# Q and K of the strided heads kept in token order, their score products reading both operands with a stride of 16 tokens

## The chip, the cores and the metric

The kernel runs on one core of a Trainium2 chip. The metric is the time of one execution on the device in microseconds (us); for the kernel before, the median of three runs is 591.43 us (590.43 to 592.25). The engines are called PE (TensorE matmuls), PEld (TensorE's weight loads, which overlap the matmuls), DVE (VectorE), ACT (ScalarE), POOL (GpSimd) and SP (SyncE, which issues most transfers).

## The reference, cut to what matters

Eight batches of eight heads, 576 tokens, head dimension 64, all in float32. A sparse attention is followed by a gated feed-forward block with a product over the token dimension:

```python
stride = 32
rel = pos[:, None] - pos[None, :]
mask_local = (rel >= 0) & (rel < stride)
mask_strided = (rel >= 0) & (pos[None, :] % stride == pos[:, None] % stride)
masks = np.stack([mask_local if h < H // 2 else mask_strided for h in range(H)], axis=0)
scores = np.where(masks[None], scale * np.matmul(q, k.transpose(0, 1, 3, 2)), -1e9)
attn = softmax(scores)
attn_out = np.matmul(attn, v)              # 8 heads side by side: x[b, token, 512]

h = gelu(x @ w_in)                         # 512 -> 1024
u, v = h[..., :512], h[..., 512:]
v_n = layernorm(v) * g_ln
v_s = einsum('ts,bsd->btd', w_sg, v_n) + b_sg
out = x + (u * v_s) @ w_out
```

Heads 0 to 3 are local (a token sees the 32 tokens up to itself), heads 4 to 7 strided (a token sees those earlier tokens whose number is the same modulo 32). The kernel groups the strided heads' tokens into 16 classes modulo 16, 36 tokens each. The score product of a class with itself is 36 by 36, and a mask then takes out half of it by parity.

## The kernel before, in words

Heads are handled in four pairs `hh` (0 and 1 local, 2 and 3 strided). The two heads of a pair lie on partitions 0 to 63 and 64 to 127, so every tile of a pair holds both.

For a pair, `qk_load` (step LQ) brings Q and K in as `raw` tiles, 32-token blocks with tokens on partitions. `qk_transpose` (step TQ, lines 425 to 437) turns each with one DVE transpose in 32 by 32 blocks into `qT` and `kT`: head dimension on partitions, 576 tokens along the row. For the strided pairs (lines 435 and 436) the transpose writes through a rearranged view, so that the 36 tokens of a class lie next to each other: inside a 32-token block its output moves on by 36 elements per token. For the local pairs it writes the row straight through.

`strided_scores` (step SS, line 490) makes 32 products per pair: 16 classes by 2 heads, each with 36 columns of `qT` as the weights and 36 columns of `kT` as the moving operand, into one tile `ss`. On the trace each float32 product is two records, so a pair has 64 matmul records and 64 weight loads, and the two heads' products stand side by side in the instruction stream on different halves of the array.

After the scores come the softmax steps: MK adds the mask (DVE, reads `ss`), MX the maximum, SB the subtraction, EX the exponential (ACT), SU the sums, ML the product with the reciprocal (POOL or DVE), then transposes of the probabilities (PS), their copy (CS, ACT) and the product with V (PV, PW) into `os`. XH and XL split the result `os` into two parts of `xt`; for strided pairs they write `xt` through the view `by_class`, which puts class-ordered columns back in token order with a step of 16 elements. XR and XD send it to DRAM for the residual.

The feed-forward part of a batch is made of products with full tiles: `v` (56 matmuls), `u` (96), `sg` (112), `o` (48 or 60), 64 or 128 weight columns, 288 or 512 moving columns.

The order of all work is written out by hand in three strings of steps: START (batch 0's attention, the weights' preparation, batch 0's feed-forward and batch 1's attention), CYCLE (batches 1 to 6: feed-forward of batch b, attention of batch b+1) and LAST (batch 7). In a CYCLE the PE's part is v, local scores, v, u, SS of pairs 2 and 3 back to back, u, sg, o with the attention's products between. TQ of pair 3 stands behind the local scores' mask, TQ of pair 2 behind the layer norm's centring (step lm). Every engine runs its own instructions in this order; no step passes another on the same engine. All calls go through one recording helper, so the profile shows nearly everything as line 81, and instructions are told apart by tiles.

Of the kernel before, what the change touches and what calls it, by code (L numbers as in the profile page):

```python
# [99 lines left out]
def tile_sparse_attention_moe(  # L100
# [17 lines left out]
    B, H, S, D = q.shape  # L118
    P = 128
    DM = H * D  # L120
    NH = DM // P
# [4 lines left out]
    NCL = 16  # L126
    TP = S // NCL
# [22 lines left out]
    def psum(name, own, other):  # L150
        banks, tag = other if alt[0] else own
        return banks.tile([P, 2, 512], F32, tag=tag, name=name)
# [4 lines left out]
    def at_tile(name):  # L157
        return psum(name, (psa, "at"), (psm, "mm"))
# [266 lines left out]
    def qk_transpose(b, hh):  # L425

        for nm in ("q", "k"):
            flat = state[b, hh, "raw" + nm].rearrange("p n d -> p (n d)")
            if nm == "k" and hh < NH // 2:
                dst = state[b, hh, "k"][:, ST : ST + S]  # L430
            else:
                tt = p2.tile([P, S + ST], F32, tag=nm + "T", name=f"{nm}T_{b}_{hh}")
                state[b, hh, nm] = tt
                dst = tt[:, 0:S]
            if hh >= NH // 2:
                dst = dst.rearrange("p (tl tb th) -> p tb th tl", tl=NCL, th=2)
            dve.transpose(dst, flat)

    def v_zeros(b, hh):
# [50 lines left out]
    def strided_scores(b, hh):  # L490
        qT, kT = state[b, hh, "q"], state[b, hh, "k"]
        ps = state[b, "s", hh] = at_tile(f"ss_{b}_{hh}")
        for rb in range(8):
            for n in range(2):
                c = 8 * n + rb
                for hp in range(2):
                    hr = slice(64 * hp, 64 * hp + 64)
                    pe.matmul(
                        ps[64 * hp : 64 * hp + TP, n, rb * TP : rb * TP + TP],
                        qT[hr, c * TP : c * TP + TP],  # L500
                        kT[hr, c * TP : c * TP + TP],
                        start=True, stop=True,
                    )

# [401 lines left out]
    def out_send(b, kk):  # L906
# [7 lines left out]
    STEPS = {  # L914

        "LQ": qk_load, "TQ": qk_transpose, "LV": v_load, "TZ": k_zeros, "LZ": v_zeros, "SL": local_scores,
        "SS": strided_scores, "MK": sm_mask, "MX": sm_max, "SB": sm_sub, "EX": sm_exp,
        "SU": sm_sum, "ML": sm_mul, "PL": local_pt, "CL": local_pt_copy, "CM": local_pt_last,
        "VA": lambda b, hh: local_pv(b, hh, range(NJ)),
# [79 lines left out]
```

## Time and profile before

| | before |
|---|---|
| median of 3 runs | 591.43 us |
| the profiled execution's own time | 591.94 us |
| its span (first to last instruction) | 590.2 us |
| mean granted TensorE clock | 0.984 |
| PE busy | 537.2 us, 91% |
| DVE busy | 412.1 us, 70% |
| ACT busy | 269.4 us, 46% |
| POOL busy | 206.4 us, 35% |

The span falls into three parts. Up to about 60 us the PE is mostly idle while weights are prepared and the first attention is made. From about 60 to 137 us the PE is mostly busy, with some waits. From 137 us on it runs almost without a break to the end. A row of the timeline gives start, duration, engine, operation, output<-inputs, shapes and count; where the engine stood idle before, a bracket tells how long and what ended it. A matmul's duration there holds its way through the pipeline, so the pace of a stream is read from the distance between starts and not from the duration of one.

### The profile page before, as it was taken

The numbers are of one execution on the slowest core, as the hardware profiler recorded it, in microseconds if no ns is written. First come the engines' busy times: TensorE is split into PE (matmuls) and PEld (weight loads), VectorE is DVE, ScalarE is ACT, GpSimd is POOL, SyncE is SP. The second block draws the span as 40 slices with busy tenths as digits, with TensorE's granted clock in tenths as the row PEclk, the third lists the DMA queues.
The fourth block names the chain that finished last, engine by engine and source line by source line (L and its number), as shares of the span: only waits on it lengthen the run. The fifth ranks groups of instructions, "written<-read, shape, count | busy, mean of one in ns | idle before, by whom it ended". The sixth has DMA issues, their size and how long they took to land.

```text
span 590.2 us, 14898 instructions
## 1 busy us (share of the span) xinstructions
PE 537.2 (91%) x6033; PEld 481.4 (82%) x6033; DVE 412.1 (70%) x676; ACT 269.4 (46%) x379; POOL 206.4 (35%) x476
## 2 busy tenths in 40 slices
PE   0344998999999999999999999999999999999996
PEld 0334787988998889978998888988998889988995
DVE  5899999768875587657875587657875587545532
ACT  2455655641572338433562337443662338434320
POOL 6354574630732035300732026310732035302310
PEclk9996799999999999999999999999999999999999
DMA  9998737786852787247832777247932781056002
GB/s 201 177 166 170 148 87 148 143 183 160 175 83 61 160 154 136 41 117 159 167 64 60 160 154 129 41 116 161 171 57 59 162 156 46 0 118 157 0 1 89
DMA packets 281061, 69.94 MB, mean 118 GB/s; under 512 B 266721, under 2 KB 266721, under 8 KB 280994
## 3 DMA queue, kind: packets, MB, share of 16 engines
q1 hardware_dynamic: 199970, 50.12, 41.7%
q10 hardware_dynamic: 81024, 18.89, 15.4%
q8 instruction: 47, 0.77, 0.6%
q14 instruction: 20, 0.16, 0.1%
HBM read 50.09 MB, written 18.87 MB: 117 GB/s over the span
## 4 chain that ended last, share of the span: by engine, by line
PE 65%; DVE 9%; DMA 6%; SPq 5%; ACT 4%; POOL 4%; issue 3%; ACTq 3%; DVEq 0%
PE sg L81 18%; PE o L81 14%; PE v L81 11%; PE u L81 11%; SPq L81 5%; DMA xd<-xs 3%; PE os L81 3%; POOL nt L81 3%; ACTq L81 3%; PE ol L81 2%; PE sa L81 2%; DMA v<-in_v_dram 1%; PE ss L81 1%; DVE cv L81 1%; ACT L81 1%
## 5 line engine op out<-in xcount | busy, mean ns | idle before, releaser
L81 PE MATMUL sg<-wsh,vg 128*128 128x288 f32 x512 | 113.1, 296 | 0.0
L81 PE MATMUL u<-xt,wih 128*128 128x288 f32 x512 | 103.9, 297 | 2.1 <-ACT u L81 2.1
L81 PE MATMUL o<-woh,vg 128*128 128x512 f32 x288 | 95.6, 397 | 0.0
L81 PEld LDWEIGHTS sg<-wsh,vg 128*128 128x128 f32 x512 | 85.6, 188 | 0.5
L81 PE MATMUL v<-wih,xt 128*128 128x512 f32 x256 | 85.0, 402 | 1.0 <-DVE xt L81 1.0
L81 PEld LDWEIGHTS u<-xt,wih 128*128 128x128 f32 x512 | 82.1, 188 | 4.0 <-ACT u L81 2.8
L81 ACT ACT_TABLE_LOAD x40 | 51.3, 1283 | 54.3 <-DMA xd<-xs 26.6
L81 PE MATMUL u<-xt,wil 128*128 128x288 f32 x256 | 75.4, 295 | 0.0
L81 PE MATMUL sg<-wsl,vg 128*128 128x288 f32 x256 | 75.4, 294 | 0.0
L81 PEld LDWEIGHTS o<-woh,vg 128*128 128x128 f32 x288 | 54.1, 188 | 11.2
L81 PEld LDWEIGHTS v<-wih,xt 128*128 128x128 f32 x256 | 48.3, 190 | 13.5 <-DVE xt L81 2.1
L81 PE MATMUL o<-wol,vg 128*128 128x512 f32 x144 | 56.3, 391 | 0.0
L81 DVE TENSOR_TENSOR ob<-o,xn 128x512 f32<-128x512 f32 x32 | 22.0, 691 | 45.4 <-PE o L81 43.0
L81 PE MATMUL v<-wil,xt 128*128 128x512 f32 x128 | 50.6, 395 | 0.0
L81 ACT CAST vg<-gt 128x576 fp32r<-128x576 f32 (+2 forms) x48 | 22.9, 509 | 60.5 <-DVE gt L81 60.5
L81 PEld LDWEIGHTS sg<-wsl,vg 128*128 128x128 f32 x256 | 48.2, 188 | 0.0
L81 PEld LDWEIGHTS u<-xt,wil 128*128 128x128 f32 x256 | 48.0, 188 | 0.0
L81 POOL TENSOR_TENSOR sms<-sms,sr 100x576 f32<-100x576 f32 x15 | 17.5, 1164 | 64.5 <-DVE sr L81 64.5
L81 DVE TENSOR_TENSOR gt<-sg,u 128x576 f32<-128x576 f32 x32 | 23.6, 738 | 22.5 <-PE sg L81 13.7
L81 DVE BATCH_NORM_STATS2 bnst<-hv 128x6 f32<-128x512 f32 (+1 forms) x40 | 27.0, 676 | 17.0 <-ACT hv L81 16.9
L81 PE MATMUL sa<-kT,qT 64*32 64x64 f32 x1024 | 16.4, 244 | 19.5 <-DVE kT L81 19.5
L81 DVE SCALAR_TENSOR_TENSOR vg<-hv,y,vg 128x512 fp32r<-128x512 f32 x32 | 22.5, 746 | 15.4 <-ACT vg L81 15.4
(144 smaller groups left out, 1079.3 us busy)
## 6 DMA issues: line engine op xcount, KB each, us to landing
rawq<-in_q_dram SPq DMA_DIRECT2D x128, 72.0 KB
rawk<-in_k_dram SPq DMA_DIRECT2D x128, 72.0 KB
xd<-xs ACTq DMA_DIRECT2D x128, 72.0 KB
xn<-xd SPq DMA_DIRECT2D x8, 1024.0 KB
out_dram<-ob ACTq DMA_DIRECT2D x32, 256.0 KB
v<-in_v_dram SPq DMA_DIRECT2D x32, 144.0 KB
v<-in_v_dram SPq DMA_DIRECT2D x64, 72.0 KB
stage<-in_moe_w_in_dram SPq DMA_DIRECT2D x8, 512.0 KB
```

The source lines that it names most:

```text
L81: ins = self.tc.keep_in_program_order(op(*args, **kwargs))
```

## The change

Q and K of the strided pairs are transposed into token order, as the local pairs' are. The score products of a class `c` then read the tokens `c`, `c + 16`, `c + 32` and so on directly from the row: both their operands, the weights and the moving one, have a step of 16 elements (64 bytes) between columns. The result `ss` is laid out as before, and nothing behind it is touched.

```diff
@@ qk_transpose
                 dst = tt[:, 0:S]
-            if hh >= NH // 2:
-                dst = dst.rearrange("p (tl tb th) -> p tb th tl", tl=NCL, th=2)
             dve.transpose(dst, flat)
@@ strided_scores
         ps = state[b, "s", hh] = at_tile(f"ss_{b}_{hh}")
+        qc, kc = (x[:, 0:S].rearrange("p (t c) -> p c t", c=NCL) for x in (qT, kT))
         for rb in range(8):
             for n in range(2):
                 c = 8 * n + rb
@@
                     pe.matmul(
                         ps[64 * hp : 64 * hp + TP, n, rb * TP : rb * TP + TP],
-                        qT[hr, c * TP : c * TP + TP],
-                        kT[hr, c * TP : c * TP + TP],
+                        qc[hr, c],
+                        kc[hr, c],
                         start=True, stop=True,
                     )
```

No instruction is added, removed or moved. On the DVE the transposes of the strided pairs keep their place and change their output shape; these rows are the place in START where TQ of pair 3 stands between a softmax's reciprocal (`sr`) and the splitting of a weight tile (`wsl`, `wst`):

```order
 L81 TENSOR_SCALAR sr_4_313<-sr_4_313 128x8
 L81 RECIPROCAL sr_4_313<-sr_4_313 128x8
-L81 STREAM_TRANSPOSE qT_3_328<-rawq_3_317 128x36x16
-L81 STREAM_TRANSPOSE kT_3_330<-rawk_3_322 128x36x16
+L81 STREAM_TRANSPOSE qT_3_328<-rawq_3_317 128x576
+L81 STREAM_TRANSPOSE kT_3_330<-rawk_3_322 128x576
 L81 TENSOR_TENSOR wsl<-wsgT_334,wsh 128x4x128
 L81 TENSOR_TENSOR wst<-wsgT_334,wsh 64x128
```

The neighbours are the same; the strided output 36 by 16 became one run of 576. The PE's list is the same row by row, since only the step inside the operands of the `ss` products differs.

## Prediction

> **What bounds the kernel now.** I read the page first (busy times and the 40 slices), then busy time by stretches, then the PE's timeline around the products that the change touches, then the waits of the PE, and at last the groups of instructions by shape. The page:
>
> ```profile
> span 590.2 us, 14898 instructions
> PE 537.2 (91%) x6033; PEld 481.4 (82%) x6033; DVE 412.1 (70%) x676; ACT 269.4 (46%) x379; POOL 206.4 (35%) x476
> PE   0344998999999999999999999999999999999996
> DVE  5899999768875587657875587657875587545532
> ```
>
> Busy time by stretches, first the preparation, then two of the loop's batches:
>
> ```profile
> 28.80:57.00 28.20, 12.87 (x224) 11.20 (x219) 27.31 (x48) 16.03 (x28) 13.82 (x13) 0.86 0.91 165
> ...
> 137.00:204.50 67.50, 67.26 (x762) 60.34 (x760) 47.65 (x76) 31.20 (x41) 20.93 (x54) 1.00 0.62 125
> 204.50:269.20 64.70, 63.93 (x747) 57.69 (x745) 45.49 (x70) 30.82 (x37) 20.74 (x53) 1.00 0.59 118
> ```
>
> The columns are PE, PEld, DVE, ACT and POOL. From 29 to 57 us DVE is full (27.31 of 28.20 us) and PE is not half busy; in the loop PE is full (67.26 of 67.50 us) and DVE has some 20 us free in a batch. So there are two rules: in the preparation a shorter DVE instruction can count; from about 137 us on only PE time counts, and a saving on DVE counts where PE waits for something behind DVE.
>
> The strided scores on PE's timeline, in START (28.54, 87.90, 94.92) and in a batch of the loop (223.31):
>
> ```profile
> 28.54 2.14 PE L81 MATMUL ss<-kT,qT 64*36 64x36 f32 x64 [4.41 <-DVE kT L81]
> ...
> 87.90 1.31 PE L81 MATMUL ss<-kT,qT 64*36 64x36 f32 x64
> ...
> 94.92 1.31 PE L81 MATMUL ss<-kT,qT 64*36 64x36 f32 x64 [1.79 <-ACT u L81]
> ...
> 100.51 0.74 PE L81 MATMUL wsgT<-ident,wsg 128*128 128x128 f32 x5 [0.90 <-DMA wsg<-in_moe_w_sg_dram]
> 223.31 2.43 PE L81 MATMUL ss<-kT,qT 64*36 64x36 f32 x128
> 225.67 0.54 PE L81 MATMUL u<-xt,wih 128*128 128x288 f32 x2
> ```
>
> In the loop 128 records start between 223.31 and 225.67, 2.36 us. Two records, one per head, stand side by side on the two halves of the array, so there are 64 steps of 36.9 ns; the work before and behind is the `u` product of the same engine, without a bracket: the block lies bare on the path. The chain that ended last holds it as a piece of its own:
>
> ```profile
> 223.38 2.36 PE ss L81 x128
> ```
>
> Six batches of the loop have this block (batches 1 to 6; the last makes no attention), and START has four blocks of 64.
>
> What PE waits for in all:
>
> ```profile
> PE ss L81 <- DVE kT L81: 7.0, 2, 4.4
> ...
> PE u L81 <- ACT u L81: 2.1, 3, 1.1
> PE ss L81 <- ACT u L81: 1.8, 1, 1.8
> ```
>
> The 7.0 us are the two blocks of batch 0, in the preparation. The 2.1 us are three batches of the loop, where the `u` product behind the scores needs a PSUM tile that ACT has not yet emptied.
>
> **The change, part by part: the DVE transposes.** A transposition into a strided output and one straight through:
>
> ```profile
> 219.80 1.25 DVE L81 STREAM_TRANSPOSE qT<-rawq 128x576 f32<-128x576 f32 x1
> 220.90 1.21 DVE L81 STREAM_TRANSPOSE kT<-rawk 128x576 f32<-128x576 f32 x1
> ...
> 239.20 0.77 DVE L81 STREAM_TRANSPOSE qT<-rawq 128x576 f32<-128x576 f32 x1
> 239.90 0.74 DVE L81 STREAM_TRANSPOSE kT<-rawk 128x576 f32<-128x576 f32 x1
> ```
>
> The second pair is the local heads' and has the very form that the strided pairs get. A pair of transposes falls from 2.46 to 1.51 us, by 0.95; sixteen pairs (8 batches, 2 strided pairs of heads) give 15.2 us of DVE time.
>
> In the loop that is 1.9 us a batch on an engine with 20 us free. For it to count, PE must wait behind it, and there it waits in three batches, 2.1 us together. The chain of one of these waits:
>
> ```profile
> 290.80 0.20 POOL y L81
> ...
> 291.02 1.34 ACT vg L81 x2
> ...
> 293.68 0.66 ACT u L81
> ...
> 294.38 3.45 PE u L81 x24
> ```
>
> ACT empties the tile late because it first waits for POOL's chain of the layer norm (step lr, which stands ahead of TQ of pair 2 in the string and so doesn't wait for it). So I take 0 there, with 2.1 us as the other end.
>
> In START four pairs stand, two of them among the full DVE work of the preparation:
>
> ```profile
> 27.17 1.22 DVE L81 STREAM_TRANSPOSE kT<-rawk 128x576 f32<-128x576 f32 x1
> 28.80 0.69 DVE L81 TENSOR_TENSOR wsl<-wsgT,wsh 128x512 fp32r<-128x512 f32 x1 [0.41 <-ACT wsh L81]
> ...
> 35.95 1.21 DVE L81 STREAM_TRANSPOSE qT<-rawq 128x576 f32<-128x576 f32 x1
> ...
> 73.08 1.20 DVE L81 STREAM_TRANSPOSE qT<-rawq 128x576 f32<-128x576 f32 x1
> ```
>
> Behind the first pair DVE had finished `kT` and stood 0.41 us for ACT; ending 0.95 us sooner it would stand 1.36 us. The second pair (35.95 us) is followed by dense work, so its 0.95 us should pass on to the end of the preparation. Two more pairs (from 73.08 us) come where PE is nearly full; what they could free are the waits of 1.79 and 0.90 us above, and the latter is for a transfer. I take 1.0 us for all of START, between 0 and 3.6 (0.95 and these two waits).
>
> **The change, part by part: the strided products.** 36 columns at a step of 64 bytes, on both operands. No matmul or weight load of this kernel reads with such a step, so the price is bounded. From below: nothing. A strided read that costs nothing is in the trace, though from PSUM: `xs<-os` reads with a step, `xs<-ol` straight.
>
> ```profile
> L81 DVE STREAM_TRANSPOSE xs<-os 128x576 f32<-128x576 f32 x16 | 12.5, 778 | 12.7 <-PE os L81 12.7
> L81 DVE STREAM_TRANSPOSE xs<-ol 128x576 f32<-128x576 f32 x16 | 12.4, 774 | 0.1
> ```
>
> From above: accesses to SBUF with the very step of 16 float32 elements, on two engines. `xt<-os` has it (ACT writes with it; DVE reads one operand and writes with it), `xt<-ol` goes straight:
>
> ```profile
> L81 DVE TENSOR_TENSOR xt<-os,xt 128x576 fp32r<-128x576 f32 x16 | 18.2, 1140 | 3.3 <-ACT xt L81 3.3
> L81 DVE TENSOR_TENSOR xt<-ol,xt 128x576 fp32r<-128x576 f32 x15 | 11.2, 749 | 4.4 <-ACT xt L81 4.2
> L81 DVE TENSOR_TENSOR xt<-ol,xt 128x64 fp32r<-128x64 f32 x1 | 0.2, 225 | 0.5 <-ACT xt L81 0.5
> L81 ACT CAST xt<-os 128x576 fp32r<-128x576 f32 x16 | 18.4, 1160 | 17.9 <-PE os L81 16.9 <-DVE xs L81 1.0
> L81 ACT CAST xt<-ol 128x576 fp32r<-128x576 f32 x15 | 9.6, 639 | 39.8 <-DVE ob L81 23.0 <-PE ol L81 16.8
> L81 ACT CAST xt<-ol 128x64 fp32r<-128x64 f32 x1 | 0.2, 188 | 0.0
> ```
>
> An element straight costs DVE (749 - 225) / 512 = 1.02 ns, and the step adds (1140 - 749) / 576 = 0.68: 1.70 ns. On ACT it is (639 - 188) / 512 = 0.88 plus (1160 - 639) / 576 = 0.90: 1.78 ns. Two engines of different pace come out within 5% of each other, which looks like a pace of the memory, one element of a new place every 1.7 to 1.8 ns, rather than one of the engine. If PE's operands come at this pace, 36 columns take 61 to 64 ns instead of the 36.9 ns that a step takes now. I take 63 ns, nearest to these rows because they share memory, step and element type with the new operands. That weights and moving columns come side by side, and both heads too, is how the stream works now: a step of 36.9 ns already holds two weight loads and two matmuls.
>
> The Trainium skill (Advanced Engine Details and Errata, section SBUF Cachelines) speaks against this change: SBUF has lines of 16 bytes, and a stream that touches a new line with each access pays; it makes no difference there between engines, or between reading and writing. In the new operands each column is in another line. The rows agree for DVE and ACT; for a PE operand no run here shows it, and the page gives no price. By it alone the sum would be the one forecast here, and a free read is excluded.
>
> The sum, against the profiled execution's 591.94 us (span 590.2 us and 1.7 us around it):
>
> - six blocks of the loop: 64 steps of 63 ns are 4.03 us, with the 0.1 us at the entry 4.15 instead of 2.36, so 6 x 1.79 = +10.7 us;
> - the wait of `u` for ACT in three of these batches: ACT's chain does not depend on the scores, PE just comes later, so the wait goes: -2.1 us;
> - START, blocks at 87.90 and 94.92 us: 32 steps more at 26 ns, 0.9 us each; the first falls into the 1.79 us wait, the second into the 0.90 us wait: 0;
> - START, the first two blocks: with the longest record (the row below) taken off, a step takes (2.14 - 0.27) / 32 = 58 ns there already, and 5 ns more a step are 0.2 us: 0;
> - the transposes: -1.0 us.
>
> ```profile
> L81 PE MATMUL ss<-kT,qT x1024: 199/199/272, 28.5 to 490.7; 64*36 64x36 f32 x171
> ```
>
> The three numbers are the shortest, median and longest record in ns. Together +7.6 us: 599.5 us for an execution such as the profiled one, and 599.0 us from the median of 591.43, which is 0.5 us lower. Own range of this case: with 61 ns a step and both gains at 2 us more, 595.5; with 5 ns a step on top of 64 ns and no gains, 6 x 64 x 32 ns = +12.3, 603.5.
>
> **The rivals.**
>
> *PE reads a column at this step as fast as before* (it ends on the other side, faster). At a step of 36.9 ns a column lasts about 1 ns, twice what the full products need:
>
> ```profile
> 217.02 6.36 PE u L81 x48
> ```
>
> 48 matmuls of 288 columns in 6.36 us are 0.46 ns a column. So the float32 products leave the read path twice the time per column, and if its limit at a new place is below 1.0 ns, nothing is lost. Then only the transposes count: -1.0 us, -5.7 at best (3.6 and 2.1 together): 590.4 us, between 585.7 and 591.4. For it speaks that slack; against it, that both engines that show the step at SBUF pay, up to 1.78 ns. The point that decides is 1.0 ns a column.
>
> *Weights and moving columns share one way into PE.* Then a step lasts 2 x 63 = 126 ns; a block of 128 grows by 64 x 89 ns = 5.7 us, six by 34.2 us, the two later blocks of START by 2.85 us each, of which the two waits take 2.7; less 2.1 and 1.0: +34 us, about 625 us. Against it: in `u`, 128 weights and 288 columns pass in 132 ns, 0.32 ns each, so both streams do come together. The Trainium skill (TensorE: Matmul & The Clock Gate, section Step-by-step: what each phase is for) gives PE two independent read ports, one per operand; by that rule this rival is out.
>
> *A part of the price only*, 45 to 50 ns a step: 64 x 6 x 8 to 13 ns = +3 to +5 us, less the same gains: 591.5 to 594.
>
> That the transposes do not get shorter can hardly be: the local pairs have the same instruction, input and output form, in the same run.
>
> **How the numbers follow.** The full price 0.60: all rows at this step in SBUF show it, but none is a PE read. The free read 0.26, for the slack. A part 0.06, the shared way 0.08. A measurement of this kernel tells about 0.3% from no change, 1.8 us. The free read is faster by more than that if over 0.8 us is gained beyond the 1.0 us, which I hold for somewhat over half: 0.16, and 0.10 the same. Of the partial case 0.04 are the same and 0.02 slower. So faster 0.16, same 0.14, slower 0.70. The range 588.5 to 603.5 leaves out the shared way (0.08), the best third of the free read (0.08) and a little above: about 0.18.
>
> **What would show it.** The strided transposes at 0.74 to 0.77 us; then each block of 128 `ss` records in the loop, from its first start to the next `u`: 4.1 us if the price is the memory's, 2.36 if the read is free, about 8 if the operands share a way. With the first, the waits of `u` for ACT should be gone and the batches of the loop about 1.8 us longer where there was none; the first two blocks of START should stay near 2.1 us. Wrong I would be with a block still at 2.4 us, or with blocks of 4.1 us and a time that does not follow them.

## The result and the profile after

The changed kernel takes 601.2 us (median of 4 runs, 600.73 to 602.17) against 591.84 us (four runs of the kernel before): a ratio of 1.0153, 95% interval 1.0124 to 1.0181. It is slower by about 9 us; forecast were 599.0 us and a range of 588.5 to 603.5. The profiled execution took 601.18 us with a span of 599.5 us, 9.2 us more than the one before.

The page of the changed kernel:

```profile
span 599.5 us, 14898 instructions
PE 548.1 (91%) x6033; PEld 493.2 (82%) x6033; DVE 401.3 (67%) x676; ACT 268.9 (45%) x379; POOL 205.4 (34%) x476
```

Over the same number of instructions, DVE is busy 10.8 us less and PE 10.9 us more. The first change is the transposes. Their group in the changed kernel (busy time, then the mean of one in ns; each group holds the local and the strided pairs):

```profile
L81 DVE STREAM_TRANSPOSE qT<-rawq 128x576 f32<-128x576 f32 x32 | 24.4, 762 | 0.0
L81 DVE STREAM_TRANSPOSE kT<-rawk 128x576 f32<-128x576 f32 x32 | 23.6, 736 | 0.2 <-DMA rawk<-in_k_dram 0.2
```

The same groups before:

```profile
L81 DVE STREAM_TRANSPOSE qT<-rawq 128x576 f32<-128x576 f32 x32 | 31.7, 992 | 0.0
L81 DVE STREAM_TRANSPOSE kT<-rawk 128x576 f32<-128x576 f32 x32 | 31.1, 971 | 0.0
```

All transposes now last what the local ones did, and the two groups have 14.8 us less (forecast 15.2). DVE's busy time falls by less, since neighbouring rows overlap and a few rows of the preparation (`stage`, `cxl`, `wol`) are 2.2 us longer in this trace. The second change is the score products, in the first block of START and in two batches of the loop:

```profile
27.54 2.31 PE L81 MATMUL ss<-kT,qT 64*36 64x36 f32 x64 [3.42 <-DVE kT L81]
...
158.50 4.37 PE L81 MATMUL ss<-kT,qT 64*36 64x36 f32 x128
162.80 0.40 PE L81 MATMUL u<-xt,wih 128*128 128x288 f32 x1
...
361.82 4.30 PE L81 MATMUL ss<-kT,qT 64*36 64x36 f32 x128
366.06 0.53 PE L81 MATMUL u<-xt,wih 128*128 128x288 f32 x2
```

A block of the loop has 4.24 us from its first start to the next `u` product (366.06 - 361.82), in every second batch 4.30 (162.80 - 158.50), that is 66 to 67 ns a step of two records with the entry, where it had 2.36 us and 36.9 ns. On the chain that ended last it stands with its full length:

```profile
361.89 4.23 PE ss L81 x126
366.13 6.55 PE u L81 x48
```

The first block of START grew little, as forecast: its 64 records lasted 2.14 us and last 2.31. And PE's waits:

```profile
PE ss L81 <- DVE kT L81: 5.2, 2, 3.4
...
PE ss L81 <- ACT u L81: 1.5, 1, 1.5
```

The row of `u` waiting for ACT, 2.1 us before, is gone: PE comes later to that place and finds the tile empty.

### The profile page after: what moved, and what is told of

Read it like the earlier page. It is cut to its first block, busy times and chain, and to the rows that moved or that the text cites. A ratio compares the mean times of both kernels' runs of the same rounds, so it can differ in the third digit from the quotient of the medians.

```text
span 599.5 us, 14898 instructions
## 1 busy us (share of the span) xinstructions
PE 548.1 (91%) x6033; PEld 493.2 (82%) x6033; DVE 401.3 (67%) x676; ACT 268.9 (45%) x379; POOL 205.4 (34%) x476
## 3 DMA queue, kind: packets, MB, share of 16 engines
q10 hardware_dynamic: 81024, 18.89, 15.2%
## 4 chain that ended last, share of the span: by engine, by line
PE 79%; DVE 6%; DMA 4%; SPq 3%; POOL 2%; issue 2%; ACT 2%; ACTq 1%; DVEq 0%; POOLq 0%
PE sg L81 17%; PE v L81 17%; PE o L81 15%; PE u L81 15%; PE ss L81 5%; SPq L81 3%; PE os L81 3%; PE ol L81 2%; PE sa L81 2%; DMA cs<-in_moe_w_out_dram 1%; PE ptl L81 1%; PE pts L81 1%; DMA stage<-in_moe_w_in_dram 1%; POOL nt L81 1%; DMA rawk<-in_k_dram 1%
## 5 line engine op out<-in xcount | busy, mean ns | idle before, releaser
L81 PE MATMUL ss<-kT,qT 64*36 64x36 f32 x1024 | 35.3, 241 | 6.8 <-DVE kT L81 5.2
L81 PEld LDWEIGHTS ss<-kT,qT 64*36 64x36 f32 x1024 | 34.1, 155 | 9.0 <-issue 7.2
```

Source lines behind the costliest of these rows:

```text
L81: ins = self.tc.keep_in_program_order(op(*args, **kwargs))
```

## The experiments

The theory to be tested: an operand that PE reads from a new place with each column comes at the pace of the memory, about 1.75 ns a column, whatever PE's own pace; this price lies bare in the loop, and the transposes give little back. The rivals were that both operands share one way, that only one of them pays, that the distance or the bank and not the new line is the cause, and, for the time, that START or the waits take more or less of it than the prediction's sum says. One helper tells the layouts apart in most kernels below:

```diff
+    def run_of(b, hh, nm):
+        return NCL                      # the changed kernel; 1 is the kernel before
...
-                dst = dst.rearrange("p (tl tb th) -> p tb th tl", tl=NCL, th=2)
+                cl = run_of(b, hh, nm)
+                if cl < NCL:
+                    dst = dst.rearrange("p (ch m cl) -> p m ch cl", cl=cl, m=TP)
...
+            x[:, 0:S].rearrange("p (ch t cl) -> p ch cl t", cl=cl, t=TP)
```

With `cl` tokens of neighbouring classes side by side, the transposes write runs of `cl` elements and the products read with a step of `cl`.

### One operand at a time

Q alone in token order (weights read with the step):

```diff
+        return NCL if nm == "q" else 1
```

> Only Q of the strided pairs is kept in token order, so the weights of the score products are read with a step of 16 elements and the moving columns side by side. Theory (each operand comes at the memory's pace by a way of its own, and the slower sets the step): a step of two records stays at 63 to 64 ns, a block of 128 records in the loop at 4.1 to 4.2 us, time 599 to 602 us. Rival 1 (both operands share one way): half the added time, a step of about 50 ns, a block of 3.3 us, 595 to 597 us. Rival 2 (only the moving operand pays, the weight load hides behind it): a step of 35 to 37 ns, 591 to 592 us.

K alone (moving columns read with the step):

```diff
+        return NCL if nm == "k" else 1
```

> Only K of the strided pairs is kept in token order, so the moving columns are read with a step of 16 elements and the weights side by side. Theory (own ways, the slower sets the step): 63 to 64 ns a step, a block of 4.1 to 4.2 us, 599 to 602 us. Rival 1 (one shared way): about 50 ns, 3.3 us, 595 to 597 us. Rival 2 (only the moving operand pays): 63 to 64 ns here as well, so that it differs from the theory only in the kernel with Q in token order.

Measured: 600.44 us, ratio 1.0148 (1.0131 to 1.0164), with Q alone; 600.31 us, 1.0143 (1.0121 to 1.0164), with K alone. The block of batch 1's loop, first with Q alone, then with K alone:

```profile
157.92 4.27 PE L81 MATMUL ss<-kT,qT 64*36 64x36 f32 x128
162.12 0.53 PE L81 MATMUL u<-xt,wih 128*128 128x288 f32 x2
```

```profile
156.56 4.24 PE L81 MATMUL ss<-kT,qT 64*36 64x36 f32 x128
160.73 0.54 PE L81 MATMUL u<-xt,wih 128*128 128x288 f32 x2
```

4.20 and 4.17 us (in all six batches 4.20 to 4.22 with Q alone, 4.17 with K alone): either operand alone costs nearly all of what both cost (4.24 to 4.30). Both rivals fall. The weight load is not hidden behind the matmul, and the two do not share one way, or one alone would have cost half. The Trainium skill's two read ports of PE, one per operand (TensorE: Matmul & The Clock Gate, section Step-by-step: what each phase is for), agree with that.

### The transposes alone

The transposes of the changed kernel, with the products reading 36 neighbouring columns:

```diff
-        qw, kw = run_of(b, hh, "q"), run_of(b, hh, "k")
+        qw, kw = 1, 1
```

> The transposes of the changed kernel alone: Q and K lie in token order, but the score products read 36 neighbouring columns, as before, and so leave out the choice of the class's tokens. Theory: transposes at 0.73 to 0.78 us, blocks of 2.36 us, and a gain between 0 and 1 us, since in the changed kernel the second stage of the first attention was 0.3 us ahead at 88 us: 590.5 to 591.8 us. Rival (the shorter DVE work shows wherever PE waited behind it, START's two waits and the three waits of the loop): -3 to -5 us, 587 to 589 us.

Measured: 589.64 us, ratio 0.9973 (0.9958 to 0.9988), between the two expectations and inside neither. Its block:

```profile
155.53 2.43 PE L81 MATMUL ss<-kT,qT 64*36 64x36 f32 x128
157.89 0.54 PE L81 MATMUL u<-xt,wih 128*128 128x288 f32 x2
```

With the reads side by side the block is back at 2.36 us, so the layout in memory alone costs PE nothing; the step of the reads does. The shorter transposes are worth about 1.6 us (0.27% of 591.5).

### How far the step must go: 2, 4, 8 and 17 elements

Runs of 2, 4 and 8 elements (`return 2`, `return 4`, `return 8` in the helper), and token order with a free element behind every 16 tokens:

```diff
-                dst = tt[:, 0:S]
+                    dst = tt[:, 0 : 17 * TP].rearrange("p (t c) -> p t c", c=17)[:, :, 0:NCL]
...
+        qc, kc = (x[:, 0 : 17 * TP].rearrange("p (t c) -> p c t", c=17) for x in (qT, kT))
```

> A layout in between: tokens c and c+1 of two neighbouring classes side by side, so the transposes write runs of 2 elements and the products read with a step of 2 elements, 8 bytes, in both operands. Theory (an operand pays for each new line of 16 bytes): two columns share a line, 0.9 ns a column or so is enough, a step of 35 to 40 ns, a block of 2.3 to 2.6 us; transposes between 0.75 and 1.2 us; time 590 to 593 us. Rival (any step above one element costs PE the full price): 63 ns, a block of 4.1 us, 599 to 602 us.

> The layout in between with runs of 4 elements: the transposes write 16 bytes at a time, the products read with a step of 4 elements, 16 bytes, in both operands, so each column lies in another line of 16 bytes. Theory (a new 16-byte line with each column costs, however near it is): a step of 63 to 65 ns, a block of 4.1 to 4.3 us in the loop, 599 to 602 us. Rival (what counts is a larger unit of memory, 32 or 64 bytes, or the distance): 35 ns or something between 35 and 63, a block of 2.4 to 3.3 us, 590 to 596 us.

> Runs of 8 elements, products read with a step of 8 elements, 32 bytes. Theory (a new 16-byte line with each column): the same 63 to 65 ns as with 16 and with 64 bytes, a block of 4.1 to 4.3 us, 599 to 602 us. Rival (a larger unit of 64 bytes, or a price that grows with the distance): between 35 and 55 ns, a block of 2.4 to 3.6 us.

> Token order with one element left free behind every 16 tokens, so the products read with a step of 17 elements, 68 bytes, in both operands: the columns no longer stand at the same place of a 64-byte unit. Theory (a new line is what costs): 63 to 66 ns a step as with 16 elements, a block of 4.1 to 4.3 us, 599 to 602 us. Rival (columns at a step of 64 bytes fall into the same bank of the memory and wait for each other): the odd step spreads them, a step of 35 to 45 ns, a block of 2.4 to 3 us, 590 to 594 us.

The same block of the loop, steps of 2, 4, 8 and 17 elements in that order:

```profile
157.47 2.44 PE L81 MATMUL ss<-kT,qT 64*36 64x36 f32 x128
159.84 0.54 PE L81 MATMUL u<-xt,wih 128*128 128x288 f32 x2
```

```profile
157.72 4.58 PE L81 MATMUL ss<-kT,qT 64*36 64x36 f32 x128
162.22 0.54 PE L81 MATMUL u<-xt,wih 128*128 128x288 f32 x2
```

```profile
157.41 4.66 PE L81 MATMUL ss<-kT,qT 64*36 64x36 f32 x128
162.01 0.53 PE L81 MATMUL u<-xt,wih 128*128 128x288 f32 x2
```

```profile
158.09 4.47 PE L81 MATMUL ss<-kT,qT 64*36 64x36 f32 x128
162.49 0.53 PE L81 MATMUL u<-xt,wih 128*128 128x288 f32 x2
```

| step, elements (bytes) | block, first start to next `u` | time, us |
|---|---|---|
| 1 (4), the kernel before | 2.36 us | 591.84 |
| 2 (8) | 2.37 us | 590.60, ratio 0.9985 (0.9969 to 1.0002) |
| 4 (16) | 4.50 us | 603.94 (one run) |
| 8 (32) | 4.60 us | 602.49 (one run) |
| 16 (64), the changed kernel | 4.24 to 4.30 us | 601.20 |
| 17 (68) | 4.40 us | 601.81 (one run) |

A step of 2 is free, one of 4 costs the full price; a step of 3 was not run, so the limit lies somewhere between 8 and 16 bytes. The Trainium skill (Advanced Engine Details and Errata, section SBUF Cachelines) has lines of 16 bytes in SBUF and asks for at least two hits on a line; the runs agree with it on a PE operand. The distance plays no part to speak of, and an odd step does not help, so it is no conflict of banks at 64 bytes. The theory held, though its blocks of 4.1 to 4.3 us are up to 0.3 us short at steps of 4, 8 and 17, and the times at steps of 4 and 8 lie above its 599 to 602 us.

The transposes with runs of 2 elements are as short as those straight through:

```profile
L81 DVE STREAM_TRANSPOSE qT<-rawq 128x576 f32<-128x576 f32 x32 | 24.5, 765 | 0.0
L81 DVE STREAM_TRANSPOSE kT<-rawk 128x576 f32<-128x576 f32 x32 | 23.6, 738 | 0.0
```

So this layout takes DVE's whole saving and pays nothing on PE. It beats the changed kernel by about 1.7% (0.9985 against 1.0153 of the kernel before), but the kernel before by no more than can be told: its interval reaches from 0.3% faster to none.

### START and the loop apart

The changed kernel's layout in batches 0 and 1 only, then in batches 2 to 7 only, then everywhere but in the last block of START (which gets its strided transposes back too):

```diff
+        return NCL if b < 2 else 1
...
+        return NCL if b >= 2 else 1
...
+        return 1 if (b, hh) == (1, 3) else NCL
```

> Token order with step-16 reads for batches 0 and 1 only, whose scores are all made in START; the loop is that of before. Theory (in START the price of the last block of scores, 1.0 us, passes on, by DVE that waits for it, and the shorter transposes give back less than that): first v product of batch 1 at 136 to 137.5 us, time +0.5 to +2.5 us, 592 to 594 us. Rival (START's own waits swallow the longer blocks and the transposes gain there, as predicted): -1.0 us, 590 to 591 us.

> Token order with step-16 reads for batches 2 to 7 only, whose scores are made in the six batches of the loop; START is that of before. Theory (six blocks longer by 1.9 us each, less the waits of u for ACT): +7.0 to +8.5 us, 598.5 to 600 us, first v product of batch 1 at 135 to 136 us as in the kernel before. Rival (the loop pays in full, the waits only move): +11 us, 602 to 603 us.

> The changed kernel with one of its sixteen blocks of 64 score records put back, that of batch 1, pair 3, the last of START (class order, transposes into the strided output). Theory (this block's 1.0 us passes on through DVE, which waits for it): that block 1.24 us instead of 2.27, first v product of batch 1 earlier than in the changed kernel by 0.8 to 1.6 us, 135.3 to 136.3 us, time 599.5 to 600.5 us. Rival (the block falls into the wait for the weight's transfer behind it): 136.5 to 137.2 us as in the two traces of the changed kernel, time unchanged.

> The changed kernel once more, unchanged, for a second trace of START. Theory (START's time up to the first v product of batch 1 is later than before by about 2 us because the last block of scores in START delays DVE): that product at 136.5 to 137.5 us again, against 135.1 us in the trace of before. Rival (START differs from run to run by a us or two on its own): anywhere between 134 and 137.5 us.

> The kernel before once more, unchanged, for a second trace of START. Theory (START is 1 to 2 us longer in the changed kernel): first v product of batch 1 at 134.7 to 135.5 us again. Rival (START differs from run to run by as much): 136 us or later.

START ends where the first `v` product of the batch behind it starts. That row in seven traces: the kernel before, the same once more, the layout in the loop only (START is that of before in these three); the changed kernel, the same once more, the layout in START only; and with the last block put back:

```profile
135.07 0.39 PE L81 MATMUL v<-wih,xt 128*128 128x512 f32 x1
```

```profile
134.80 0.39 PE L81 MATMUL v<-wih,xt 128*128 128x512 f32 x1
```

```profile
134.74 0.39 PE L81 MATMUL v<-wih,xt 128*128 128x512 f32 x1
```

```profile
137.11 0.39 PE L81 MATMUL v<-wih,xt 128*128 128x512 f32 x1
```

```profile
136.46 0.39 PE L81 MATMUL v<-wih,xt 128*128 128x512 f32 x1
```

```profile
136.13 0.39 PE L81 MATMUL v<-wih,xt 128*128 128x512 f32 x1
```

```profile
135.34 0.39 PE L81 MATMUL v<-wih,xt 128*128 128x512 f32 x1
```

The first three have 134.87 us on average, the next three 136.57: START is 1.7 us longer, 1.1 to 2.4 in any pair. With one block of 64 put back most of that is gone (135.34).

Two traces of the other layouts limit what this shows. With runs of 2 elements, where the block is as short as before, the same row starts at 136.12 us: in that trace the granted clock was 0.65 from 74 to 78 us, where it was 1.00 in the seven above, and PE was 1.5 us behind the kernel before by the second pair's block (89.38 against 87.90). So one trace can be late for another reason. And with K alone, where the last block of START is nearly as long as in the changed kernel, START is hardly longer:

```profile
94.78 2.21 PE L81 MATMUL ss<-kT,qT 64*36 64x36 f32 x64 [0.74 <-ACT u L81]
...
135.17 0.39 PE L81 MATMUL v<-wih,xt 128*128 128x512 f32 x1
```

The same block in the kernel where it is put back:

```profile
95.78 1.31 PE L81 MATMUL ss<-kT,qT 64*36 64x36 f32 x64 [1.50 <-ACT u L81]
```

The block's start matters as much as its length. It starts at 94.78 to 94.92 us in the three traces with START of before and with K alone, and at 95.37 to 95.86 us in the three with the changed layout in START and with the block put back. A long block that starts early leaves START 0.3 us longer, a short one that starts late 0.5 us (one trace each), and both together 1.7 us.

What is left to the end of the span is the loop with the last batch: 455.1, 453.1 and 453.6 us with the loop of before (590.2 - 135.07, 587.9 - 134.80, 589.7 - 136.13), 462.4, 462.7 and 463.1 us with the new one (599.5, 599.2 and 597.8 us of span): 453.9 and 462.7 on average, 8.8 us more.

The times: 592.12 us for START only, ratio 1.0007 (0.9979 to 1.0034); 599.82 us for the loop only, 1.0131 (1.0107 to 1.0155); 600.31 us with the last block put back, 1.0130 (1.0110 to 1.0150); 600.9 us for the changed kernel and 589.63 us for the kernel before in one run each. START's 1.7 us are inside the first interval (-1.2 to +2.0 us); in time alone they would not have been seen. By the ratios the two parts are +0.4 and +7.8 us, less than the traces' 1.7 and 8.8: the traces are few, and the second of the kernel before is one of its fastest executions.

How the last block of START reaches the end shows the chain of the changed kernel:

```profile
94.25 1.08 ACT u L81 x2
...
95.37 2.36 PE ss L81 x64
...
97.76 0.75 DVE sms L81
98.52 0.76 DVE sms L81
...
99.32 0.44 DVE cxl L81
```

the same piece of the chain before:

```profile
94.92 1.34 PE ss L81 x64
...
96.28 0.75 DVE sms L81
```

and DVE's waits for that block, before and after:

```profile
DVE sms L81 <- PE ss L81: 0.2, 1, 0.2
```

```profile
DVE sms L81 <- PE ss L81: 1.8, 1, 1.8
```

DVE stands in its list before the mask `sms` of this block, and the weights' preparation (`cxl`) is queued behind it. The block ends at 97.7 us and DVE goes on 1.5 us later than before; 0.45 us of that is the block's later start (95.37 against 94.92), the rest its length. Why it starts later is not shown. PE waits there for ACT to empty `u`, and just ahead of that ACT's four issues of `xd<-xs` take 4.32 to 4.42 us in the four traces with the late start and 3.17 to 3.77 in the four with the early one.

## Why the prediction was right

It was right on direction and size, and right on the mechanism that carried the sum; two terms of the sum were off, START and the waits, and partly made up for each other.

- **The price of a step.** Forecast 63 ns, 4.15 us a block; measured 4.17 to 4.22 us with one operand strided and 4.24 to 4.30 with both. Six blocks are about +11.4 us (three at 1.88, three at 1.94 over 2.36) where +10.7 was forecast. The guess that PE comes at the pace of the strided accesses on DVE and ACT (1.70 and 1.78 ns an element) held: (4.20 us less 0.1 at the entry) / 64 / 36 is 1.78 ns a column. That the memory sets this pace is inferred from three engines that agree; the runs show the price, and that it depends on the step and hardly on the operand. The runs with a single operand show that the two operands come side by side, as was assumed.
- **The first two blocks of START.** Forecast 0.2 us and set at 0, measured 0.17 us for each (2.31 against 2.14). The strided step is about the same there as in the loop, (2.31 us less a longest record of 0.28) / 32 = 63 ns, though the straight step differs (58 and 36.9 ns): a price that does not follow PE's own pace.
- **The waits of `u` for ACT.** Forecast -2.1 us, and they are gone. But they are not a constant of the kernel before. Its second trace has one of them:

```profile
PE u L81 <- ACT u L81: 0.3, 1, 0.3
```

Its loop is 2.0 us shorter than that of the first trace, so the sum of the loop (+8.6 forecast, +8.8 measured over three traces each) is as exact as that allows. More went than this row: from the block's start to the first `sg` product the six batches take 8.87 to 10.22 us in the first trace of before and 8.83 to 9.41 in the second, but 10.69 to 10.76 in both traces of the changed kernel. That is the shortest of before, 8.83, and the block's 1.88 to 1.94 us: no wait is left there, however many there were.
- **START.** Here two steps failed. "The first falls into the 1.79 us wait": that wait stayed (1.51, 1.38 and 1.29 us against 1.79, 1.27 and 1.60), because ACT emptied `u` later too. "The second into the 0.90 us wait: 0" looked at PE alone. PE's wait behind the last block was for a transfer, but DVE waited for the block itself, and the preparation of weights queued behind it passed the delay on. START is 1.7 us longer and not 1.0 shorter. That the block's length has a part in it is shown by putting the block back (1.1 and 1.8 us earlier than the two traces of the changed kernel), and that its later start is needed as well by K alone (135.17 us), by one trace each. Why it starts later, and how much DVE's saving in START is worth beside it, stays open.
- **The transposes.** Forecast -1.0 us for all; alone they are worth 1.6 us (0.7 to 2.5 by the interval of the ratio). In the trace of that run START is 0.7 us shorter than the average of before (134.14 us) and the rest, where the forecast took 0, 1.3 us (452.6), within the 2 us by which the rest of before varies. The free read, the rival on the other side, would so have given about 590 us; it decided at 1.0 ns a column, and the column came at 1.78. The shared way is refuted by the runs with one operand.

Together: 11.4 for the blocks, 2.0 for START of this pair of traces (137.11 - 135.07) and 4.2 less in the loop's waits and small gaps make the 9.2 us between the two profiled executions (the 4.2 is what is left over; 3.3 of it lie between the block and the first `sg` product, where six batches took 56.2 us and take 64.3, the rest was not followed). Against the forecast's 10.7, -1.0 and -2.1 the blocks are 0.7 dearer, START is 3.0 worse and the waits give 2.1 more: that the total is nearer than START's term is luck.

Two bounds of the prediction do not come out of their own terms: 591.43 and 12.3 us are 603.7 and not 603.5, and a part of the price, 3 to 5 us less 3.1, is 591.4 to 593.3 and not 591.5 to 594. Nothing hangs on either.

## What to carry to other kernels

A stride on a matmul operand is paid by the engine that is the bound, in every product, while a strided write ahead of it is paid once and here on an engine with time to spare: look who is full before moving a rearrangement. Here the strided accesses of DVE (1.70 ns an element) and ACT (1.78) on the same memory were a good estimate for PE's (1.78 ns a column) in absolute time, and the loss is largest where PE would otherwise be fastest. If both sides are to be cheap, keep two neighbouring elements of 4 bytes together: a step of 2 was free for the weights, for the moving columns and for the transposes that wrote them.

## What the runs showed that was not expected

- The weight load pays as much as the moving operand: 4.20 to 4.22 against 4.17 us a block with either alone, although weight loads overlap matmuls. The pace of loads is here as hard a bound as that of the products.
- Steps of 16 and 32 bytes are dearer than one of 64: 4.50 and 4.60 against 4.24 to 4.30 us a block, with 68 bytes between them at 4.40. Nothing here explains that.
- A DVE transpose that writes runs of only 8 bytes at a distance is as fast as one that writes a whole row (765 and 738 ns against 762 and 736), where runs of 4 bytes took 1.21 to 1.25 us.
